# A two-layer decode kernel on one core: three unit loads as 120 and 8 rows, and part of a fourth in sixteen row groups

## The chip, the core and the metric

The kernel runs on one core of one Trainium2 chip. A core has a matmul engine (TensorE, PE in the profile), a vector engine (VectorE, DVE), a scalar engine (ScalarE, ACT), GpSimd (POOL) and SyncE (SP), and 16 DMA engines that move data between the chip's memory (HBM) and the core's SBUF. SBUF has 128 partitions, which are called rows here. The metric is device microseconds (us) of one execution.

## The reference

Two rounds of attention over a cache and of a gated feed-forward block, for two sequences of one new token each. All data are float32.

```python
def _A_ref(x, k_cache, v_cache, wq, wo):
    q = (x @ wq).reshape(B, Sq, H, Dh).transpose(0, 2, 1, 3)
    scores = jnp.einsum("bhqd,bhkd->bhqk", q, k_cache) * (Dh ** -0.5)
    p = _softmax(scores, axis=-1)
    o = jnp.einsum("bhqk,bhkd->bhqd", p, v_cache)
    return o.transpose(0, 2, 1, 3).reshape(B, Sq, H * Dh) @ wo
...
x = x + _A_ref(_layernorm(x, axis=-1), A_k_cache, A_v_cache, A_wq, A_wo)
x = x + _B_ref(_layernorm(x, axis=-1), B_W_gate, B_W_up, B_W_down)
x = x + _A_ref(_layernorm(x, axis=-1), A_k_cache, A_v_cache, A_wq, A_wo)
x = x + _B_ref(_layernorm(x, axis=-1), B_W_gate, B_W_up, B_W_down)
```

`_B_ref` is `(relu(x W_gate) * (x W_up)) W_down`. B is 2, D 448, H 16, the cache length 4096, the head size 256, F 1792. So K and V are 32 matrices each of 4096 x 256 (4 MB), one for each pair of head and sequence, and they are read in both rounds.

## The kernel before

**Tiling.** A matrix of K or V for a pair (h, b) is laid out as 128 rows of 32 KB: each row holds 32 consecutive cache positions. It is cut along the row into four parts (`c` = 0 to 3), *units* of 128 rows x 8 KB, 1 MB. All loads go into one SBUF tile, `arena`, which has room for 27 units: six blocks of four neighbouring units and three single ones (class `Arena`, lines 35 to 62). The weights of a head (`h`, query and output projection together) and those of the feed-forward block (`in` x 7, `out` x 4) take a unit each, with rows of 7 KB (two of the `out` have 5.25 KB).

**The order of loads** is fixed before the kernel starts: the list `pending` (lines 177 and 178). In the first attention the pairs go from (0, 0) to (15, 1), in the second one backwards. Behind the K of a pair stands the V of the pair before it. A whole matrix is loaded by one DMA of 4 MB (`grouped`), except at the ends of each attention, where a DMA loads one unit: the last 12 entries of each attention (`ENDS`), and the first ones of the second. The last 12 of the first attention are K of (15, 1), V of (15, 0) and V of (15, 1), four units each. The last 12 of the second are K of (0, 0), V of (0, 1) and V of (0, 0). Behind them come the 7 + 4 feed-forward weights. 21 units of K and V that the first attention has loaded last, and the weights of its last head, stay in the arena for the second one (`keep`).

**Issue.** `pump` (lines 110 to 128) takes the head of the list as soon as the arena has room for it and issues its DMA on SP (line 124). `release` gives a unit back and pumps again. Only the very last load of the kernel is cut in two, by columns. SP issues nothing else but these loads and one half of the output, in the order of the list. Each DMA signals its landing on one of eight semaphores, taken in turn.

**Compute.** For each pair `score` or `score_block` multiplies K with the query (VectorE line 355, ScalarE line 360, VectorE line 364), softmax goes over GpSimd (line 405) and ScalarE, and `weigh` (line 432) has TensorE multiply the probabilities with V, unit by unit. `project` (line 475) adds the head's output. `ffn` follows the attention: `proj` (line 538) needs the `in` weights, line 620 the `out` weights. Each weight's unit is released when it was used, and with so many units kept, the last loads of the feed-forward wait for such releases.

Of the kernel before, what the change touches and what calls it, by code (L numbers as in the profile page):

```python
# [14 lines left out]
B, D, H, S, DH, F = 2, 448, 16, 4096, 256, 1792  # L15
P = 128
# [11 lines left out]
ENDS = 12  # L28
HASTE = 5
BY_ACT = 3  # L30
EPS = 1e-5
SCALE = DH**-0.5

# [32 lines left out]
def two_layers(  # L66
# [10 lines left out]
    nc = tc.nc  # L77
# [16 lines left out]
    pending = []  # L94
# [3 lines left out]
    def source(key, n):  # L98
        kind, name, c = key
        if kind in "kv":  # L100
            h, b = name
            rows = (k_cache if kind == "k" else v_cache)[b, h]
            return rows.rearrange("(p t) d -> p (t d)", t=NT)[:, c * UNIT : (c + n) * UNIT]
        if kind == "h":
            return w_head[name]
        if kind == "in":
            return w_in[c]
        return w_out[:, (14 * c + 2) // 4 * D : (14 * c + 16) // 4 * D]

    def pump():  # L110
        while pending:
            (kind, name, c), n = pending[0]
            last = at_of.get((kind, name, c - 1)) if kind in "kv" else None
            at = units.take(n, kind, last)
            if at is None:
                return
            pending.pop(0)
            src = source((kind, name, c), n)
            dst = arena[:, at * UNIT : at * UNIT + src.shape[1]]
            parts = [0, src.shape[1]]  # L120
            if not pending:
                parts[1:1] = [src.shape[1] - D]
            for i, j in zip(parts, parts[1:]):
                nc.sync.dma_start(dst[:, i:j], src[:, i:j])
            for k in range(n):
                at_of[kind, name, c + k] = at + k
            if n == NC:
                blocks.add((kind, name))
# [5 lines left out]
    def release(*key):  # L134
        units.free.add(at_of.pop(key))
        pump()
# [45 lines left out]
    y_rows = junk[:, : D // 2], consts.tile([P, D // 2], F32, name="y_row")  # L182
    nc.scalar.dma_start(row[:B, :D], x.rearrange("b s d -> (b s) d"))
    pump()


# [13 lines left out]
    eps_t = consts.tile([P, 1], F32, name="eps_t")  # L200
    nc.vector.memset(eps_t, EPS)

# [72 lines left out]
    def attention(order, after, begun):  # L275
# [93 lines left out]
        def score(u, c):  # L369
# [6 lines left out]
            found = s_of[u][:, c * CT : (c + 1) * CT]  # L376
            by_act = 0 if kept else BY_ACT
            if ahead and u < HASTE:
                by_act = 0 if u == 0 else CT // 2
            whole = CT if by_act == BY_ACT else by_act  # L380
            if by_act:
# [300 lines left out]
def build(nc, shapes):  # L682
    import concourse.tile as _tile

    args = [
        nc.dram_tensor(f"in_{n}_dram", s, F32, kind="ExternalInput").ap() for n, s in shapes.items()
    ]
    for i, (shape, _) in enumerate(_OUTS):
        args.append(nc.dram_tensor(f"out_{i}_dram", shape, F32, kind="ExternalOutput").ap())
    with _tile.TileContext(nc) as tc:  # L690
        two_layers(tc, *args)
# [12 lines left out]
```

## Time and profile before

| | |
|---|---|
| median of 3 runs | 1328.2 us (1326.89 to 1329.47) |
| the profiled execution | 1330.6 us |
| its span, first to last instruction | 1328.8 us |
| busy: DVE, PE, ACT, POOL | 1004.3, 589.1, 317.4, 106.6 us |
| read from HBM | 562.56 MB, 423 GB/s over the span |
| loads of V by single units | 27, 1024 KB each |
| loads of K by single units | 20, 1024 KB each |

The profile's page shows the span in 40 slices of 33.2 us. A digit is a share in tenths, 9 being 90% or more. The chain that ended last is followed backwards from the last instruction: at each step to what released it. A DMA in the chain counts from its issue to its landing, so that it holds the time in the queue behind other loads too. The timeline of SP gives the start of an issue; neighbouring issues of one kind are merged into one row, whose length runs from the first issue to the end of the last. The windows by stage give the share of the 16 DMA engines that was busy in a stretch, and what was moved.

### The profile page before, as it was taken

The numbers are of one execution on the slowest core, as the hardware profiler recorded it, in microseconds if no ns is written. First come the engines' busy times: TensorE is split into PE (matmuls) and PEld (weight loads), VectorE is DVE, ScalarE is ACT, GpSimd is POOL, SyncE is SP. The second block draws the span as 40 slices with busy tenths as digits, with TensorE's granted clock in tenths as the row PEclk, the third lists the DMA queues.
The fourth block names the chain that finished last, engine by engine and source line by source line (L and its number), as shares of the span: only waits on it lengthen the run. The fifth ranks groups of instructions, "written<-read, shape, count | busy, mean of one in ns | idle before, by whom it ended". The sixth has DMA issues, their size and how long they took to land.

```text
span 1328.8 us, 9585 instructions
## 1 busy us (share of the span) xinstructions
PE 589.1 (44%) x3090; PEld 192.1 (14%) x3090; DVE 1004.3 (76%) x908; ACT 317.4 (24%) x1353; POOL 106.6 (8%) x192
## 2 busy tenths in 40 slices
PE   2434434344244442444585544434244343443437
PEld 2111111111011110112131111111011111111112
DVE  4997877878778787786719888877878778777791
ACT  2221221212212122120015622222212222222131
POOL 0130000000000000000001232000000000000010
PEclk9666566665666766767686677666676665666669
DMA  9999999999999999999999999999999999999998
GB/s 403 429 430 431 431 428 434 431 432 428 430 434 431 429 431 429 435 428 429 417 392 354 429 434 427 436 426 432 428 434 429 432 427 435 427 434 427 434 415 334
DMA packets 30589, 563.18 MB, mean 424 GB/s; under 512 B 3398, under 2 KB 3532, under 8 KB 10316
## 3 DMA queue, kind: packets, MB, share of 16 engines
q1 hardware_dynamic: 30532, 562.58, 99.3%
q8 instruction: 24, 0.39, 0.1%
q14 instruction: 25, 0.20, 0.0%
q10 hardware_dynamic: 8, 0.01, 0.0%
HBM read 562.56 MB, written 0.00 MB: 423 GB/s over the span
## 4 chain that ended last, share of the span: by engine, by line
DMA 70%; DVE 20%; PE 5%; POOL 2%; issue 2%; ACT 1%; DVEq 0%; SPq 0%; POOLq 0%; ACTq 0%
DMA arena<-in_k_cache_dram 47%; DMA arena<-in_w_head_dram 16%; DVE arena L355 10%; DVE scores L364 6%; DMA arena<-in_v_cache_dram 4%; DMA arena<-in_w_out_dram 2%; DVE arena L394 2%; POOL top L405 2%; DVE arena L385 2%; DMA arena<-in_w_in_dram 1%; PE pq L317 1%; PE acc L475 1%; ACT arena L387 1%; DVE row L448 1%; PE pf L538 0%
## 5 line engine op out<-in xcount | busy, mean ns | idle before, releaser
L355 DVE TENSOR_TENSOR arena<-arena 128x4096 f32<-128x4096 f32 x104 | 459.7, 4420 | 206.5 <-DMA arena<-in_k_cache_dram 206.5
L432 PE MATMUL po<-arena,probs 128*2 128x512 f32 x2048 | 317.9, 769 | 108.4 <-DMA arena<-in_v_cache_dram 98.6
L364 DVE TENSOR_REDUCE scores<-arena 128x24 f32<-128x6144 f32 x54 | 352.8, 6533 | 0.0
L456 PE MATMUL small<-ri,row 128*128 128x1 f32 x256 | 62.1, 346 | 453.9 <-DVE row L448 453.9
L360 ACT ACTIVATE arena<-arena 128x256 f32<-128x256 f32 x432 | 173.4, 403 | 280.2 <-DVE arena L355 280.2
L456 PEld LDWEIGHTS small<-ri,row 128*128 128x128 f32 x256 | 56.6, 308 | 515.4 <-DVE row L448 515.4
L410 ACT ACTIVATE nm<-top,nsr 128x1 f32<-128x1 f32 x64 | 18.9, 295 | 380.5 <-POOL top L405 380.5
L405 POOL PARTITION_ALL_REDUCE top<-mx x64 | 54.9, 858 | 614.2 <-DVE mx L403 613.0
L432 PEld LDWEIGHTS po<-arena,probs 128*2 128x2 f32 x2048 | 55.5, 99 | 319.7 <-issue 299.6
L475 PE MATMUL acc<-arena,oT 128*2 128x448 f32 x128 | 51.0, 895 | 111.9 <-DVE oT L465 111.9
L317 PE MATMUL pq<-arena,xs 128*33 128x256 f32 x174 | 76.4, 607 | 40.0 <-DMA arena<-in_w_head_dram 40.0
L360 ACT ACTIVATION_READ_ACCUMULATOR arena<-arena 128x1 f32 x432 | 81.1, 188 | 0.0
L333 POOL PARTITION_BROADCAST arena<-arena x58 | 27.7, 546 | 500.7 <-ACT arena L329 488.1
L329 ACT ACTIVATE arena<-pq 33x256 f32<-33x256 f32 x29 | 10.9, 377 | 208.0 <-PE pq L321 208.0
L448 DVE SCALAR_TENSOR_TENSOR row<-po,lead,row 128x256 f32<-128x256 f32 x64 | 30.7, 479 | 27.7 <-ACT row L445 27.4
L445 ACT ACTIVATE row<-po,lead 128x256 f32<-128x256 f32 x64 | 29.6, 463 | 54.3 <-PE po L432 54.3
L317 PEld LDWEIGHTS pq<-arena,xs 128*33 128x33 f32 x174 | 25.4, 162 | 109.1 <-issue 94.5
L387 ACT ACTIVATE arena<-arena 128x256 f32<-128x256 f32 x88 | 35.4, 404 | 17.4 <-DVE arena L385 17.1
L394 DVE SCALAR_TENSOR_TENSOR junk<-arena,pq 128x256 f32<-128x256 f32 x64 | 26.9, 420 | 8.3 <-DMA arena<-in_k_cache_dram 6.3
L385 DVE TENSOR_TENSOR arena<-arena 128x1024 f32<-128x1024 f32 (+1 forms) x20 | 32.8, 1641 | 0.0
L417 POOL PARTITION_ALL_REDUCE total<-rs x64 | 24.7, 386 | 61.7 <-ACT probs L413 61.7
L321 PE MATMUL pq<-arena,xs 128*33 128x128 f32 x116 | 29.1, 402 | 0.0
(124 smaller groups left out, 346.6 us busy)
## 6 DMA issues: line engine op xcount, KB each, us to landing
arena<-in_k_cache_dram SPq DMA_DIRECT2D x56, 4096.0 KB, 44.9
arena<-in_v_cache_dram SPq DMA_DIRECT2D x55, 4096.0 KB, 53.1
arena<-in_w_head_dram SPq DMA_DIRECT2D x31, 896.0 KB, 41.9
arena<-in_v_cache_dram SPq DMA_DIRECT2D x27, 1024.0 KB, 19.9
arena<-in_k_cache_dram SPq DMA_DIRECT2D x20, 1024.0 KB, 14.0
arena<-in_w_in_dram SPq DMA_DIRECT2D x14, 896.0 KB, 19.0
arena<-in_w_out_dram SPq DMA_DIRECT2D x4, 896.0 KB, 8.9
arena<-in_w_out_dram SPq DMA_DIRECT2D x3, 672.0 KB, 8.9
```

The lines of the kernel that those rows point to most:

```text
L317: nc.tensor.matmul(q, xs[:, c, :], w[:, c * DH : (c + 1) * DH], start=(c == 0), stop=False)
L355: nc.vector.tensor_mul(some, some, q_of[u][:, None, :].to_broadcast([P, 2 * CT, DH]))
L360: nc.scalar.activation(kt[:, t, :], kt[:, t, :], AF.Copy, accum_out=s_of[u][:, t : t + 1])
L364: nc.vector.reduce_sum(s_of[u][:, CT:], kt[:, CT:, :], axis=AX.X)
L385: nc.vector.tensor_mul(some, some, q_of[u][:, None, :].to_broadcast([P, whole, DH]))
L387: nc.scalar.activation(kt[:, t, :], kt[:, t, :], AF.Copy, accum_out=found[:, t : t + 1])
L394: nc.vector.scalar_tensor_tensor(junk if kept else kt[:, t, :], kt[:, t, :], 1.0, q_of[u], op0=ALU.mult, op1=ALU.mult, accum_out=found[:, ...
L405: nc.gpsimd.partition_all_reduce(mx_of[u], mx, P, RED.max)
L432: nc.tensor.matmul(po_of[u][32 * t : 32 * t + 2, :], p_of[u][:, n : n + 2], vt[:, 2 * t * DH : (2 * t + 2) * DH], start=(c == 0), stop=(c ...
L448: nc.vector.scalar_tensor_tensor(row[:, :DH], po_of.pop(u)[:, DH:], lead[:, 1:2], row[:, :DH], op0=ALU.mult, op1=ALU.add,)
L456: nc.tensor.matmul(pT_of[u][:, c : c + 1], row[:, c * P : (c + 1) * P], r_of[u], start=True, stop=True,)
L475: nc.tensor.matmul(acc[at : at + B], oT_of[h][:, c, :], wo[:, c * D : (c + 1) * D], start=(n < 3), stop=(n >= n_u - 3),)
```

## The change

A new function `boxes` gives the pieces in which a load is issued, each a range of rows and one of columns. Three single units are loaded as rows 0 to 119 and rows 120 to 127: parts 0 and 1 of the K of (15, 1), near the end of the first attention, and part 0 of the V of (0, 0), near the end of the second. A fourth, part 1 of the V of (15, 0) near the end of the first attention, is loaded as all rows without their last 64 columns (256 B), and then these 64 columns in groups of 15, 14, 13 and so on to 1 rows, and the last 8 rows: 17 loads. The bytes loaded, the places they go to and the order of the units are the same, and nothing is changed in the compute.

```diff
+FEWER = {("k", (H - 1, B - 1)): 2, ("v", (0, 0)): 1}
+STAIRS = ("v", (H - 1, 0), 1)
...
+    def boxes(kind, name, c, n, width):
+
+        cols, every = slice(0, width), slice(0, P)
+        if not pending:
+            return [(every, slice(0, width - D)), (every, slice(width - D, width))]
+        if n == 1 and (kind, name) in FEWER and c < FEWER[kind, name]:
+            return [(slice(0, 120), cols), (slice(120, P), cols)]
+        if n == 1 and (kind, name, c) == STAIRS:
+            ends = [sum(range(16 - i, 16)) for i in range(16)] + [P]
+            steps = [(slice(i, j), slice(width - P // 2, width)) for i, j in zip(ends, ends[1:])]
+            return [(every, slice(0, width - P // 2))] + steps
+        return [(every, cols)]
...
-            parts = [0, src.shape[1]]
-            if not pending:
-                parts[1:1] = [src.shape[1] - D]
-            for i, j in zip(parts, parts[1:]):
-                nc.sync.dma_start(dst[:, i:j], src[:, i:j])
+            for rows, cols in boxes(kind, name, c, n, src.shape[1]):
+                nc.sync.dma_start(dst[rows, cols], src[rows, cols])
```

## The prediction

> **What bounds the kernel now.** I read the page first: the slices and queues, then the chain that ended last.
>
> ```profile
> DMA  9999999999999999999999999999999999999998
> GB/s 403 429 430 431 431 428 434 431 432 428 430 434 431 429 431 429 435 428 429 417 392 354 429 434 427 436 426 432 428 434 429 432 427 435 427 434 427 434 415 334
> q1 hardware_dynamic: 30532, 562.58, 99.3%
> DMA 70%; DVE 20%; PE 5%; POOL 2%; issue 2%; ACT 1%; DVEq 0%; SPq 0%; POOLq 0%; ACTq 0%
> ```
>
> The 16 DMA engines are busy for 99.3% of the span with the loads of one queue, SyncE's (SP). Only slices 20 to 22 (the feed-forward stage between the layers) and the last one move clearly less. So the time is the stream of loads, and a pause put into that stream lengthens the kernel, unless a later pause swallows it. The change touches loads near the end of each layer. There I asked for the chain of waits between 590 and 800 us (columns: start, us, what):
>
> ```profile
> 559.10 44.51 DMA arena<-in_k_cache_dram
> 603.63 41.26 DMA arena<-in_k_cache_dram
> 644.96 20.61 DMA arena<-in_v_cache_dram
> 665.61 1.08 PE po L432 x8
> ...
> 671.95 3.41 PE pf L538 x32
> ...
> 676.42 1.64 PE pf L538 x16
> ...
> 679.72 8.92 DMA arena<-in_w_out_dram
> ```
>
> and for SP's timeline over the same stretch, with two narrow windows of it behind (start, us from the first to the last of the row, what, how many):
>
> ```profile
> 559.10 0.33 SPq L124 DMA_DIRECT2D arena<-in_k_cache_dram  x1
> 559.52 0.38 SPq L124 DMA_DIRECT2D arena<-in_v_cache_dram  x1
> 573.63 0.33 SPq L124 DMA_DIRECT2D arena<-in_w_head_dram  x1
> 578.41 0.33 SPq L124 DMA_DIRECT2D arena<-in_k_cache_dram  x1
> 582.54 0.33 SPq L124 DMA_DIRECT2D arena<-in_v_cache_dram  x1
> 592.12 11.85 SPq L124 DMA_DIRECT2D arena<-in_k_cache_dram  x4
> 613.41 31.88 SPq L124 DMA_DIRECT2D arena<-in_v_cache_dram  x8
> 647.45 26.58 SPq L124 DMA_DIRECT2D arena<-in_w_in_dram  x7
> ```
>
> ```profile
> 649.94 0.33 SPq L124 DMA_DIRECT2D arena<-in_w_in_dram  x1
> ```
>
> ```profile
> 653.27 0.33 SPq L124 DMA_DIRECT2D arena<-in_w_in_dram  x1
> ```
>
> Put the two views side by side. The load issued at 559.10 lands at 559.10 + 44.51 = 603.61, and 603.63 is the next issue in the chain. Count SP's rows from 559.10: 559.52, 573.63, 578.41, 582.54, then four K units of which the last starts at 592.12 + 11.85 - 0.33 = 603.64. That is the eighth load behind. Again: 603.63 + 41.26 = 644.89, and the eighth V unit behind it starts at 613.41 + 31.88 - 0.33 = 644.96. So **a load is issued only when the load eight places earlier has landed**: no more than eight are in flight, whatever their size. SP's waits between 592 and 660 us agree: landings of K and V loads hold it there 13 times (columns: total us, times, longest):
>
> ```profile
> SPq L124 <- DMA arena<-in_v_cache_dram: 29.9, 7, 9.4
> SPq L124 <- DMA arena<-in_k_cache_dram: 20.4, 6, 9.3
> ```
>
> Before the change the eight are 1 MB units or 0.9 MB weights, about 20 us of queue (the chain's 20.61), and two issues, 647.45 and 649.94, lie 2.49 us apart, which is what one unit takes. The limit costs nothing as long as every place is filled with a large load.
>
> **Part 1: the sixteen small loads.** The fourth unit is v(15, 0), part 1, the second of the eight V units. It becomes one load of 7.75 KB rows, then sixteen loads of 256 B rows (15, 14 and so on to 1, then 8 rows). The three loads of 120 + 8 rows are separate; two of them, k(15, 1) parts 0 and 1, stand just ahead. With a for 120 rows and b for 8, the order is then k0a, k0b, k1a, k1b, k2, k3, v0, v1 (the large piece), small 1 to 16, v2, v3, and so on. Eight places in flight:
>
> - Small 1 to 7 wait for k0a to v0. They are issued while v1 is still in the queue and cost nothing.
> - Small 8 waits for v1 itself. Before the change the load eight behind v1 is the second w_in, issued at 649.94, so v1 has landed just before that. At that moment only small 1 to 7 are in the queue, 84 rows of 256 B (15 + 14 + 13 + 12 + 11 + 10 + 9), 21 KB; against 1 MB in 2.49 us that is nothing. **The queue is empty.**
> - Small 9 to 16 and then v2 follow. Their eight-earlier loads are small and long or just landed, so SP's pace of issue sets the time: nine steps.
>
> A step is the distance of two issues that wait for nothing: 559.10 to 559.52 is 0.42. The bounds stand in SP's timeline of the first 60 us:
>
> ```profile
> 3.64 0.62 SPq L124 DMA_DIRECT2D arena<-in_k_cache_dram  x1
> 4.31 0.56 SPq L124 DMA_DIRECT2D arena<-in_v_cache_dram  x1
> ...
> 39.04 0.33 SPq L124 DMA_DIRECT2D arena<-in_v_cache_dram  x1
> 39.41 0.43 SPq L124 DMA_DIRECT2D arena<-in_w_head_dram  x1
> ```
>
> 0.37 (39.04 to 39.41) and 0.67 (3.64 to 4.31). I take 0.42, the row nearest in place: v2 is issued at 649.94 + 9 x 0.42 = 653.72 (653.3 to 656.0 with the bounds). What a 1 MB unit needs on an empty queue shows once, in the pause after the feed-forward stage; the second fence is the answer for this one load:
>
> ```profile
> 700.77 0.33 SPq L124 DMA_DIRECT2D arena<-in_k_cache_dram  x1
> ```
>
> ```profile
> DMA to landing us min/median/max: 4.8/4.8/4.8
> ```
>
> So v2 lands at 653.72 + 4.8 = 658.5. Before, the load eight behind v2 is the third w_in, issued at 653.27, so v2 landed just before that. The stream is **5.2 us** late. The lower bound is a restart at the bare 2.49 us: 653.3 + 2.49 - 653.27 = 2.5. The upper one is 656.0 + 4.8 - 653.27 = 7.5.
>
> Nothing hides it. Every later load (five V units, the w_in) stands in line behind v2, and the compute engines wait at the end of that line: the last V unit lands at 644.96 + 20.61 = 665.57 and PE starts on it at 665.61, then projects, and the feed-forward matmuls follow at 671.95. The w_out load at 679.72 is issued only when the feed-forward releases a unit, so the pause in slices 20 to 22 moves along and swallows nothing. PE's own wait for v1 (all seventeen landings instead of one) ends before v2's, so it adds nothing. The small loads' own transfer is inside the pause.
>
> **Part 2: 120 + 8 rows.** A row of 8 KB costs its engine 2.49 / 8 = 0.31 us, if the 128 rows are 8 on each of 16 engines. In the first layer, whatever the two split units gain on the slowest engine ends in the pause, where all engines run empty: counted as nothing. At worst v1 lands 0.6 us later (two extra rows on the slowest engine), which the bounds above hold. In the second layer v(0, 0) part 0 is followed by units without any pause, so it reaches the end. There the loads' last stretch, in the windows by stage (last two columns: DMA share, GB/s), and the chain's last landing:
>
> ```profile
> 1323.00:1323.50 0.50, 1.00 0.30 115
> 1323.50:1324.00 0.50, 1.00 0.10 36
> 1324.00:1324.50 0.50, 1.00 0.06 22
> ```
>
> ```profile
> 1308.62 15.73 DMA arena<-in_w_out_dram
> ```
>
> The engines end one after the other. A share of 0.06 is one engine of 16; 0.30 is five. The last one ends at 1308.62 + 15.73 = 1324.35, the one before it at about 1323.5 to 1323.8 (0.10 is 1.6 engines over that half us). Relieving the last engine by eight rows (2.5 us) gains therefore at most about 0.8 us, for then the next one is last; if the last one instead gets one of the extra eight rows, the end is 0.3 us later. Middle of -0.8 and +0.3: **-0.3 us**. One more load in flight there leaves seven large ones, over 17 us of queue, so it never runs empty.
>
> Which engines lose rows no row of the profile tells. [...]
>
> **Sum.** Against the profiled execution (span 1328.8, 1330.6 with what lies around it): +5.2 - 0.3 = +4.9, so 1335.5. That execution was 2.4 above the median of the runs, 1328.2, to which I add the same: **1333.1 us** (+0.37%). With the bounds, 1328.2 + 2.5 - 0.8 = 1329.9 to 1328.2 + 7.5 + 0.3 = 1336.0.
>
> **The rivals.**
>
> *The relief pays and nothing runs empty (not slower).* The engines end apart, so unloading the slowest one shortens each layer's stream. For it: the share that falls from 0.30 to 0.06 over the last 1.5 us; against it: the chain, where the landing eight earlier released the issue. It would need the small loads to be issued without that wait, all before v1 has landed; it decides as soon as the pause is under 1.6 us. Price: -0.8 in each layer, 1326.6 us. [...] Chance 0.13.
>
> *The rows pile up.* If 120 rows went to eight engines, fifteen each, a split unit would cost them 7 x 0.31 = 2.2 us more: +2.2 in the second layer, up to 4.4 in the first ahead of v1, so up to 1333.1 + 6.6 = 1339.7. Nothing in the trace of before speaks for it, as all its loads have 128 rows. Chance 0.04.
>
> *The feed-forward stage swallows part of it.* If the loads of the second layer's first units were ahead of their need, the delay would shrink by what slices 20 to 22 hold idle. The chain's 0.04 us between landing and PE at 665.6 speaks against it. At half of 5.2, 1330.5 us. Chance 0.05.
>
> **How the numbers follow.** Forecast 0.78, rivals 0.13, 0.04 and 0.05. About 0.2% (2.7 us) is what a measurement here can tell from no change. Slower by more: most of the forecast and the piling rows, 0.78; within: the first rival, the third and the forecast's low end, 0.19; faster by more: 0.03. The range is the forecast's own with a little above and down to the median of before, 1328.2 to 1336.5; outside lie the first rival, the piling rows and a small rest.
>
> **What would show it.** Right: on SP's timeline, a row of small V loads with the seventh at about 647, the eighth at about 650, nine steps of some 0.4, and v2 near 653.7; a DMA share near zero at 651 to 654; the PE's last po group near 670.8 instead of 665.61, and everything after it as late. At the end, the stretch at a share of 0.06 gone or shorter. Wrong: small loads issued back to back before 645, no hole in the DMA share at 650, or a v1 that lands clearly earlier or later than 649.9. A step much over 0.67 would make it slower than the range.

## The result, and the profile after

| | before | after |
|---|---|---|
| median | 1328.84 us (1326.89 to 1330.79) | 1349.89 us (1348.51 to 1351.61) |
| ratio, 95% interval | | 1.016 (1.0146 to 1.0173) |
| profiled execution, span | 1330.6, 1328.8 us | 1349.36, 1347.6 us |

The change makes the kernel 21 us slower; the two executions that were profiled lie 18.8 us apart. The prediction, 1333.1 us and at most 1336.5, had the sign and a quarter of the size. The page of the changed kernel shows where to look: its slices and the load queue.

```profile
DMA  9999999999999999999799999999999999999997
GB/s 400 435 432 430 428 428 432 430 430 430 431 429 433 432 431 432 430 427 364 259 414 401 427 426 439 430 429 428 432 430 432 430 432 431 425 436 429 427 355 316
...
q1 hardware_dynamic: 30809, 562.58, 98.9%
```

The DMA engines are as busy as before, 98.9% against 99.3%, but three slices move less: 364, 259 and, next to the last, 355 GB/s, where before 429, 417 and 415 stood. **Busy and slow** is a sign of its own; an empty queue shows as a lower share (0.02 from 660 to 663 below). The windows by stage separate the two. First the end of the first layer, then that of the second (columns: stretch, length, granted clock of TensorE, share of the 16 DMA engines, GB/s).

```profile
620.00:626.00 6.00, 1.00 1.02 437
...
630.00:638.00 8.00, 0.50 0.94 195
638.00:646.00 8.00, 0.75 1.02 226
...
656.00:660.00 4.00, 0.50 0.08 28
660.00:663.00 3.00, 0.59 0.02 3
663.00:667.00 4.00, 0.86 0.85 304
667.00:671.00 4.00, 0.50 1.01 420
```

```profile
1298.00:1300.00 2.00, 0.50 1.00 418
...
1302.00:1304.00 2.00, 0.50 1.02 209
...
1312.00:1314.00 2.00, 1.00 0.99 395
```

There are two kinds of loss. From 656 to 663 the share is next to nothing: the pause that was forecast, though it comes 5 to 9 us later. From 630 to 646, and again in the second layer (209 GB/s at 1302; at 1312 it is back at 395), all engines are busy and move half of what they moved at 620. GB/s divided by the share is the rate at full use: 437 / 1.02 = 428, and 195 / 0.94 = 207, 209 / 1.02 = 205. A row of 8 KB that takes 0.31 us at the first takes about 0.63 us at the second. The trace's single packets say the same: an 8 KB packet took 0.31 us (median) from 1296 to 1300 and 0.62 us from 1302 to 1306. Only the second kind of loss is there in the second layer, where nothing but one unit in 120 + 8 rows was changed.

SP's timeline of the changed kernel, with three narrow windows, shows the pause:

```profile
591.97 23.85 SPq L138 DMA_DIRECT2D arena<-in_k_cache_dram  x6
625.16 40.43 SPq L138 DMA_DIRECT2D arena<-in_v_cache_dram  x24
```

```profile
659.59 0.62 SPq L138 DMA_DIRECT2D arena<-in_v_cache_dram  x2
```

```profile
662.55 0.35 SPq L138 DMA_DIRECT2D arena<-in_v_cache_dram  x1
```

```profile
667.35 0.33 SPq L138 DMA_DIRECT2D arena<-in_w_in_dram  x1
```

The eighth small load is issued at 659.59, when v1 has landed (before: 649.94, so 9.7 us late from the slow rows). v2 is issued nine steps later, at 662.55, that is 0.33 us a step. The load eight behind v2 is issued at 667.35, where it was 653.27: v2 is 14.1 us late, 9.7 from the slow rows and 4.4 from the pause.

The chain of the changed kernel, 590 to 800 us, answers to the one shown of before:

```profile
663.00 8.23 DMA arena<-in_v_cache_dram
671.28 1.93 PE po L446 x8
...
675.29 3.52 PE po L446 x16
...
687.98 3.21 PE pf L552 x32
...
695.55 9.00 DMA arena<-in_w_out_dram
...
710.12 8.29 DVE arena L408 x48
```

The feed-forward's first matmuls start at 687.98 against 671.95, 16.0 us late: PE gets the V units in a bunch after the pause, and works them off with half the clock (0.50 in the window at 667 to 671). But the second layer's first VectorE work starts at 710.12, only 12.2 us late; the same group in the chain of before:

```profile
697.92 8.29 DVE arena L394 x48
```

What differs stands in the windows of the two feed-forward stages (here with the busy time of PE, PEld, DVE, ACT and POOL ahead of the clock), first after, then before:

```profile
700.00:712.00 12.00, 9.69 (x67) 5.63 (x68) 3.82 (x23) 2.81 (x7) 0.00 (x0) 1.00 1.02 422
```

```profile
684.00:700.00 16.00, 13.99 (x63) 8.20 (x64) 3.94 (x25) 2.82 (x7) 0.00 (x0) 0.68 0.93 386
```

The granted clock was 0.68 there before and is 1.00 after, so the matmuls between the w_out weights and the first scores take less time: from the landing of the weights to that VectorE work it is 710.12 - 704.55 = 5.57 us after and 697.92 - 688.64 = 9.28 before. That gives back 3.7 of the 3.8 us. At the end of the kernel, the chain's last load:

```profile
1326.84 15.71 DMA arena<-in_w_out_dram
```

It is issued 18.2 us late (before: 1308.62), so 6.0 us come from the second layer.

### The profile page after: what moved, and what is told of

It is laid out like the page before. It is cut to its first block, busy times and chain, and to the rows that moved or that the text cites. A ratio compares the mean times of both kernels' runs of the same rounds, so it can differ in the third digit from the quotient of the medians.

```text
span 1347.6 us, 9613 instructions
## 1 busy us (share of the span) xinstructions
PE 588.6 (44%) x3090; PEld 189.7 (14%) x3090; DVE 1004.6 (75%) x908; ACT 317.4 (24%) x1353; POOL 110.1 (8%) x192
## 3 DMA queue, kind: packets, MB, share of 16 engines
q1 hardware_dynamic: 30809, 562.58, 98.9%
## 4 chain that ended last, share of the span: by engine, by line
DMA 67%; DVE 23%; PE 4%; another core or an unknown queue 2%; issue 2%; POOL 1%; ACT 1%; SPq 0%; DVEq 0%; POOLq 0%; ACTq 0%
DMA arena<-in_k_cache_dram 50%; DVE arena L369 11%; DMA arena<-in_w_head_dram 9%; DVE scores L378 7%; DMA arena<-in_v_cache_dram 4%; DMA arena<-in_w_out_dram 2%; DVE arena L408 2%; DVE arena L399 2%; DMA arena<-in_w_in_dram 1%; POOL top L419 1%; PE pq L331 1%; PE acc L489 1%; ACT arena L401 1%; DVE row L462 1%
## 5 line engine op out<-in xcount | busy, mean ns | idle before, releaser
L446 PE MATMUL po<-arena,probs 128*2 128x512 f32 x2048 | 324.9, 774 | 119.3 <-DMA arena<-in_v_cache_dram 112.4
L424 ACT ACTIVATE nm<-top,nsr 128x1 f32<-128x1 f32 x64 | 18.8, 294 | 383.6 <-POOL top L419 383.6
L431 POOL PARTITION_ALL_REDUCE total<-rs x64 | 28.4, 444 | 61.7 <-ACT probs L427 61.7
```

The costliest lines, as they stand in the source:

```text
L446: nc.tensor.matmul(po_of[u][32 * t : 32 * t + 2, :], p_of[u][:, n : n + 2], vt[:, 2 * t * DH : (2 * t + 2) * DH], start=(c == 0), stop=(c ...
```

## The experiments

Unless said otherwise, an experiment is the changed kernel with other settings of the two tables that choose the units. Times are medians beside runs of the kernel before on the same chip.

### The two parts alone

```diff
-FEWER = {("k", (H - 1, B - 1)): 2, ("v", (0, 0)): 1}
+FEWER = {}
```

> The small loads alone, all units in 128 rows but the fourth. Theory (the queue runs empty): v1 lands near 649.9 as before, the eighth small load is issued then, v2 nine steps of 0.33 later at about 652.9 and lands at about 657.7 instead of 653.2, so 4 to 5 us more: about 1333 us, and 8 KB rows at 0.31 us throughout. Rival (the small loads cost nothing, the whole 20 us are the split units): 1328 to 1329 us. Rival (small loads slow the rows of their neighbours too): rows of 0.5 us or more around 640 to 650 and over 1338 us.

Measured: 1334.95 us against 1328.77, ratio 1.0051 (1.0035 to 1.0067), 6.2 us. The windows, and the issues of the eighth small load, of v2 and of the load eight behind v2:

```profile
640.00:644.00 4.00, 0.93 1.01 422
644.00:648.00 4.00, 0.50 0.59 240
648.00:650.00 2.00, 0.50 0.10 35
650.00:653.00 3.00, 0.50 0.02 3
653.00:656.00 3.00, 0.50 0.69 233
```

```profile
649.94 0.27 SPq L138 DMA_DIRECT2D arena<-in_v_cache_dram  x1
```

```profile
652.88 0.36 SPq L138 DMA_DIRECT2D arena<-in_v_cache_dram  x1
```

```profile
657.66 0.33 SPq L138 DMA_DIRECT2D arena<-in_w_in_dram  x1
```

Here the share falls with the GB/s (240 / 0.59 = 407 is full rate): an empty queue, not slow rows. v1 lands at 649.94 as before, v2 is issued 2.94 us later and lands 4.8 us after that, 657.66 - 653.27 = 4.4 us late. The part costs more than that and more than the 4 to 5 us expected. The windows show where to look: the share that is missing adds up to 4 x 0.41 + 2 x 0.90 + 3 x 0.98 + 3 x 0.31 = 7.3 us of all engines, from 644 on. The engines that had finished their rows of v1 stood idle while the last one still ran until 649.9.

```diff
-STAIRS = ("v", (H - 1, 0), 1)
+STAIRS = None
```

> The three units in 120 + 8 rows, without the small loads. [...] Rival (only the pause costs): 1328 to 1330 us.

Measured: 1343.71 us, ratio 1.0116 (1.0093 to 1.0139), 14.9 us. The two parts add up: 6.2 + 14.9 = 21.1, the whole change's 21.

```diff
-FEWER = {("k", (H - 1, B - 1)): 2, ("v", (0, 0)): 1}
-STAIRS = ("v", (H - 1, 0), 1)
+FEWER = {("v", (0, 0)): 1}
+STAIRS = None
```

> Only the unit in the second layer in 120 + 8 rows. [...] If the cost came from the state that the first layer's changes leave behind: 1328 us.

Measured: 1334.49 us, ratio 1.0048 (1.0026 to 1.007), 5.7 us for one unit in 120 + 8 rows; by difference 9.2 us for the two in the first layer. The windows ahead of the slow stretch and in it:

```profile
1280.00:1285.00 5.00, 0.50 1.02 423
1285.00:1297.00 12.00, 0.71 1.02 247
```

A 1 MB unit passes in 2.5 us, yet the slow time lasts 12 us. 12 x (1 - 247 / 423) = 5.0 us of transfer is lost there, nearly the whole cost. In these 12 us nearly three units passed (12 x 247 = 2964 KB), and only one of them was split: the 128-row loads beside it are slowed too.

### An empty queue

```diff
-FEWER = {("k", (H - 1, B - 1)): 2, ("v", (0, 0)): 1}
-STAIRS = ("v", (H - 1, 0), 1)
+FEWER = {("v", (H - 2, 1)): 1}
+STAIRS = None
```

> One unit, part 0 of the V of (14, 1), in 120 + 8 rows, in the second layer where it is loaded into an empty queue (landed 4.9 us after its issue before). [...] Rival (it is only the mixing with 128-row loads in the queue that conflicts, or the engines' getting out of step): rows of 0.31 us, landing as before.

Measured: 1331.4 us, ratio 1.0023 (1.0012 to 1.0035), 2.6 us. The windows ahead of the unit and in it:

```profile
702.00:703.50 1.50, 1.00 1.00 425
704.00:709.00 5.00, 0.67 1.07 224
```

The queue was not empty: the K unit ahead, issued at 699.57, still moved, and 128-row units were issued behind at 705.03 and 708.10. The 120 rows landed 9.7 us after their issue; the whole unit took 4.9 us in the profile of before. So the rate is halved (425 to 224 GB/s) without a full queue, but this run doesn't settle whether the mixing with 128-row loads is needed.

### What about the 120 + 8 rows is slow?

Three rivals: an uneven number of engines, the rows' places in HBM (a V unit's rows lie 32 KB apart), and the rows' places in SBUF. All three runs change the second layer alone.

```diff
-            return [(slice(0, 120), cols), (slice(120, P), cols)]
+            return [(slice(0, 112), cols), (slice(112, P), cols)]
```

> The unit of the second layer as 112 + 16 rows, both numbers that 16 engines divide. [...] Rival (count: a load on 15 or 8 engines is what slows): 1328 to 1329.5 us, rows of 0.31 us.

Measured: 1333.2 us against 1328.55, ratio 1.0037 (1.0026 to 1.0048).

```diff
-            return [(slice(0, 120), cols), (slice(120, P), cols)]
+            return [(slice(0, 64), cols), (slice(64, P), cols)]
```

> The same unit as 64 + 64 rows. [...] Rival (count): 1328 to 1329.5 us.

Measured: 1333.35 us, ratio 1.0041 (1.0027 to 1.0055). The windows of the 112 + 16 rows and of the 64 + 64 rows:

```profile
1283.00:1295.00 12.00, 0.67 1.02 238
```

```profile
1284.00:1296.00 12.00, 0.72 1.03 218
```

The same slow 12 us. All 16 engines are busy in it (shares of 1.02 and 1.03), and 64, 112 and 16 can all be shared evenly by 16. The counts of packets agree. A load leaves, besides its rows, packets of 4 bytes: 3394 of them in the trace of before, 16 for each of its 212 loads and two for the output. The trace of the changed kernel has 149 more: one for each of the 128 rows of 256 B in the small loads, and 7 for each of the three split units. Read as one packet for each engine that takes part, which is the author's reading and stands in no view, they tell how many engines a load uses. The split runs have as many rows, so it is what their counts add:

```profile
q1 hardware_dynamic: 30548, 562.58, 99.5%
```

This is the run with 112 + 16 rows, 16 packets more than the 30532 of before: 16 + 16 - 16. The run with 64 + 64 rows has the same count. The run with 120 + 8 rows in the second layer has 30539, 7 more: 15 + 8 - 16. By this reading a load on 15 or 8 engines isn't what slows: with 16 for every load, 112 + 16 rows cost 4.7 us and 64 + 64 rows 4.8 all the same.

```diff
+FEWER = {("in", ""): 1}
...
-        if n == 1 and (kind, name) in FEWER and c < FEWER[kind, name]:
+        if len(pending) < 12 and n == 1 and (kind, name) in FEWER and c < FEWER[kind, name]:
```

> Instead of the V unit, the first feed-forward weight of the second layer in 120 + 8 rows. Its rows of 7 KB lie one behind the other in HBM; a V unit's rows lie 32 KB apart. [...] Rival (the rows 32 KB apart collide at their source when the engines take them in another order): 1328 to 1329.5 us.

Measured: 1332.89 us, ratio 1.0033 (1.002 to 1.0045), 4.3 us.

```profile
1290.00:1298.00 8.00, 0.64 1.01 422
1299.00:1308.00 9.00, 1.00 1.02 248
```

Rows that lie one behind the other in HBM are slowed alike, so the 32 KB pitch isn't it either.

### The place in SBUF

This run shows one load size in two orders of rows: always 16 rows of 8 KB in a load.

```diff
+FEWER = {("v", (H - 2, 1)): 2}
...
+            rows = range(0, P, 16) if c == 0 else range(8)
+            return [(slice(i, i + 16) if c == 0 else slice(i, P, 8), cols) for i in rows]
```

> In the second layer, where the queue is empty around 703, part 0 of the V of (14, 1) as eight loads of 16 neighbouring rows, and part 1 as eight loads of every eighth row (r, r + 8, and so on). Every load has one row for each of 16 engines and the same bytes. [...] Rival (anything that counts engines, loads or bytes but not the place in SBUF): the same row time in both.

Measured once, 1335.42 us beside 1327.74. Counted by the packets, part 0 (neighbouring rows) ends at about 708 and part 1 (every eighth row) begins there, with some engines earlier and some later.

```profile
702.00:704.00 2.00, 0.75 0.99 156
704.00:706.00 2.00, 0.50 0.98 172
706.00:708.00 2.00, 0.50 0.62 152
708.00:710.00 2.00, 0.55 0.60 164
```

At 420 GB/s for full use and 0.31 us a row, 156 / 0.99 = 158 makes 0.83 us a row in part 0 and 172 / 0.98 = 176 makes 0.75; in part 1, 164 / 0.60 = 273 makes 0.48. A row is slower among its neighbours. In part 1 the queue wasn't always full (share 0.60), and read and written rows go together here. The next run crosses them: it reads neighbours and writes every eighth row in part 0, and the other way round in part 1. It leaves the rows of these two parts of V permuted, so only its times are of use.

```diff
+            near, far = [slice(i, i + 16) for i in range(0, P, 16)], [slice(i, P, 8) for i in range(8)]
+            return [((b, a) if c == 0 else (a, b), cols) for a, b in zip(near, far)]
```

> The loads of d1_16_rows crossed, and in the other order: part 0 as eight loads that read 16 neighbouring rows and write every eighth one, then part 1 as eight loads that read every eighth row and write 16 neighbouring ones, so the rows of these two parts of V are permuted. In d1 a row took about 0.81 us where neighbours were written (and read, and loaded first), 0.47 us where every eighth was. [...] Rival (the rows read decide): 0.8 in part 0, 0.5 in part 1. Rival (whichever part goes first into the queue is slow): 0.8 in part 0 too.

Measured once, 1334.42 us beside 1328.21. Most of part 0 lies in 702 to 706 and most of part 1 in 708 to 712, with the turn at about 707:

```profile
702.00:704.00 2.00, 0.96 0.94 201
704.00:706.00 2.00, 0.50 0.81 184
...
708.00:710.00 2.00, 0.50 1.05 152
710.00:712.00 2.00, 0.83 0.97 160
```

201 / 0.94 = 214 makes 0.61 us a row and 184 / 0.81 = 227 makes 0.58, against 152 / 1.05 = 145, 0.90, and 160 / 0.97 = 165, 0.79. The slow part is now the second one, with a share of 0.81 or more in both. The single packets agree: medians of 0.56 us at 702 to 706 and 0.87 at 708 to 712, and in the run before 0.74 at 702 to 706 and 0.46 at 708 to 712. For these loads it isn't the rows read and not the order: **the rows written in SBUF decide.** From 708 to 711 only loads of 16 rows were in flight: the K unit ahead had landed at 705.0, and the next 128-row load was issued at 711.84. So the mixing with 128-row loads isn't needed either.

Every load of 16 rows has 16 packets of 4 bytes beside its rows: the run before has 30756 packets, 30532 + 2 x (8 x 16 - 16). So rows written next to each other took 0.75 to 0.90 us and rows written eight apart 0.48 to 0.61, with as many packets of the same sizes; 128-row loads keep 0.31 us where no other shape is in flight (1296 to 1300 in the changed kernel). What makes neighbours slow is not shown.

That the place written is also what slows 120 + 8, 112 + 16 and 64 + 64 rows is the author's estimate: by GB/s and share a row took 0.54 to 0.63 us in their slow stretches, against 0.31. No run shows it, and no view tells which engine takes which rows.

### How the two costs grow

```diff
+FEWER = {("v", (0, 0)): 4}
+STAIRS = None
```

> All four units of the V of (0, 0) in 120 + 8 rows, in the second layer. Theory (half the rate as long as any engine is in such a load, and the engines are up to 4 us apart): the first unit carries the entry and the exit, each further one 2.5 to 3.5 us, in all 11 to 16 us: 1340 to 1345 us. Rival (a fixed cost for each split unit, 5.7 us): about 23 us, 1351 us.

Measured: 1342.83 us against 1327.74, ratio 1.0111 (1.0095 to 1.0128), 15.1 us. The slow stretch:

```profile
1287.00:1313.00 26.00, 0.69 0.99 222
```

Four units lose 15.1 us where one loses 5.7, so each further one costs 3.1. By the expectation the first one carries the entry and the exit. That fits engines that reach a unit at different times, of which those that are in it slow the others, but no run shows it by itself.

The small loads, sixteen replaced by eight and by four, with all units in 128 rows:

```diff
+            ends = [*range(0, P + 1, 16)]
```

> No unit split by rows but the fourth one's last 64 columns, in eight loads of 16 rows instead of sixteen. Theory (the queue runs empty from the landing of v1 until SP has issued its way to v2, 0.33 us a step): two steps instead of nine, so 2.3 us less than the sixteen: v2 lands at about 655.3, and 1330.5 to 1333 us in all. Rival (any small load waiting for v1 costs the whole pause): 1334 to 1335 us.

Measured: 1331.87 us against 1327.74, ratio 1.0028 (1.0016 to 1.004). v2 follows the eighth small load by one step, not by the two that the expectation counted. The two are issued at 649.99 and 650.40, the load eight behind v2 at 655.12. The windows up to then and the issues:

```profile
646.00:650.00 4.00, 0.50 0.25 93
650.00:652.00 2.00, 0.50 0.42 76
```

```profile
649.99 0.78 SPq L138 DMA_DIRECT2D arena<-in_v_cache_dram  x2
```

```profile
655.12 0.33 SPq L138 DMA_DIRECT2D arena<-in_w_in_dram  x1
```

v2 is 655.12 - 653.27 = 1.9 us late instead of 4.4: 2.5 us for eight steps less, 0.31 each. The run costs 4.1 us all the same (2.1 to 5.3 by the interval of its ratio). The missing share is 4 x 0.75 + 2 x 0.58 = 4.2 us here and 7.3 with sixteen small loads, for costs of 4.1 and 6.2: these follow the idle time of all engines better than the lateness of v2, 1.9 and 4.4.

```diff
+            ends = [0, 32, 64, 96, P]
```

> No unit split by rows but the fourth one's last 64 columns, in four loads of 32 rows instead of sixteen. Theory (the queue runs empty only because sixteen small loads fill all eight places): v2 waits for a load two units ahead of v1, nothing runs empty, 1328 to 1329.5 us. Rival (each small load costs the stream a part of the 6 us, or a split by rows slows here too): 1330 us or more.

Measured: 1328.95 us against 1328.55, ratio 1.0 (0.9991 to 1.0009). With four small loads v2 waits for k2, three units ahead of v1 (the expectation says two). There is always a large load in flight, and nothing is lost:

```profile
640.00:655.00 15.00, 0.66 1.02 416
```

## Why the prediction was wrong

- **What bounds the kernel**: right. The chain of loads and the limit of eight in flight hold: the eighth small load leaves when v1 lands, 649.94 in the run with the small loads alone, the moment that the prediction took.
- **Part 1, the small loads**: right, and near in size. The step is 0.33 us, below the lower bound of 0.37 (0.42 was taken); v2 lands 4.4 us late instead of 5.2; the part alone costs 6.2 us (4.7 to 8.9 by the interval of its ratio). Dose and absence agree: eight small loads cost 4.1 us, four nothing. What the sum left out: it began the pause when the last engine had finished v1, but the engines end one after the other, as the prediction itself read at the kernel's end, and the first ones were idle from about 645 on.
- **"Nothing hides it", and the pause in slices 20 to 22 "swallows nothing"**: not quite. PE adds to the delay, with its bunch of V units, and the feed-forward gives 3.7 us back, because TensorE had the full clock there. The clock is in the windows; why it was higher is not shown.
- **Part 2, the step that failed**: "A row of 8 KB costs its engine 2.49 / 8 = 0.31 us", and with it "-0.3 us" and "counted as nothing". The price of a row in a 128-row load was carried over to loads of other shapes, and only the number of rows on each engine was counted. In 120 + 8, 112 + 16, 64 + 64 and eight times 16 rows a row takes 0.5 to 0.9 us, and the 128-row loads beside them are slowed too. No run shows the term of -0.3 us, neither eight rows less on the last engine nor one more; in its place the runs showed 14.9 us more: 5.7 in the second layer and, by difference, 9.2 in the first, which the prediction counted as nothing. The prediction said itself that all loads of before have 128 rows. That was the place for a wide range: no row of before bounded the price of another shape.
- **The rivals**: "the rows pile up" came nearest, with up to 6.6 us for fewer engines with more rows each. Its mechanism, few engines with many rows of 0.31 us each, fell with the packet counts (read as 15 engines for 120 rows and 16 for 112) and with the windows, where all engines are busy (a share of 1.02 at 247 and at 238 GB/s) and each row is slow; 112 + 16 rows cost 4.7 us. The relief of the slowest engine didn't show in any run; whether the relieved engine was the last one stays open, because no run relieves an engine without also slowing all of them. None of the rivals weighed where in SBUF the rows are written.

## What to carry to other kernels

A load's price belongs to its shape: before you cut a 128-row load by rows, measure one such load, and cut by columns where you can (the 7.75 KB rows of v1, all 128 in one load, took 0.30 us each, the median in the trace of the changed kernel). Here a share of busy DMA engines near 1 with half the GB/s meant slow rows, and a low share an empty queue; read the two side by side. And where the number of loads in flight is limited, a run of small loads as long as that limit empties the queue: eight cost 4.1 us here, four nothing.

## What was not expected of the hardware

- One 1 MB unit in 120 + 8 rows lowers the rate of all 16 engines from 423 to 247 GB/s for 12 us, nearly five times as long as the unit itself takes (2.5 us).
- Rows written next to each other are slower than rows eight apart, with the same number and size of packets: 0.75 to 0.90 us against 0.48 to 0.61.
- SP issued the small loads of 1 to 8 rows every 0.33 us, faster than any pair in the profile of before (0.37). Behind one of 16 rows the next issue came 0.41 us later (649.99 to 650.40).
- After the longer pause TensorE was granted a clock of 1.00 at the end of the feed-forward stage instead of 0.68, which gave back 3.7 us.
